# Block 0's constants made by GpSimd, one bias loaded later, and a new order for the prologue's last 382 steps

## The chip, the cores and the metric

The kernel runs on one core of one Trainium2 chip. The metric is the device time of one execution in microseconds (us); the median of three runs stands for it. One execution was also recorded by the hardware profiler, and all rows below come from that one.

## The reference

Two stages follow each other. The first is attention with 4 batches, 8 heads, 768 positions and a head size of 64. A query sees the keys less than 16 positions away, and 24 pooled keys (the maximum over each block of 32 keys, with log 32 added to the score). The pooled values are the means of the same blocks. The second is a gated MLP on the 3072 tokens.

```python
scores_l = scale * q @ k.T            # only |i-j| < 16 is kept
scores_s = scale * q @ k_sum.T + log(32)
a = softmax(concat(scores_l, scores_s))
x = a @ concat(v, v_sum)              # 3072 x 512 after joining the heads
g = x @ w_gate                        # 512 x 1536
out = (silu(g) * (x @ w_val)) @ w_out # 1536 x 512
```

The MLP's weights come as 64-bit floats, and the kernel turns them into 32-bit ones on the chip.

## The kernel before, in words

The 3072 tokens are cut into six blocks of 512. A block's attention is done for four pairs of heads, u = 0 to 3, and its MLP in twelve slices, j = 0 to 11, of 128 hidden channels. A matmul of the MLP is made of three in a rounded format: each factor is split into a high part and a rest, and high x rest, rest x high and high x high are added. So `gate(k,j)` and `val(k,j)` (line 654, tiles g and v) are 12 matmuls of 128x512 each, and `down(k,j)` (line 701, tiles acc) is 12 more.

For each pair, attention is a chain over the engines: `scores` (or `sw` and `sp` in block 0) on TensorE, `ttr0` and `ttr1` (L512, bias and maximum) on VectorE, `exp0` and `exp1` on ScalarE, `rcp` and `nrm` (the division by the sum), `tr0` and `tr1` (L570, transposes on TensorE, against an identity), `pt0` and `pt1` (their copies), `out` (L619, tile xo) on TensorE, `split` on ScalarE and `rest` on VectorE, which make the high part xh and the rest xl for the MLP.

Each weight slice passes through eight steps: `w_load` (DMA), `w_abs` (L217, ScalarE), `w_c1`, `w_c2`, `w_s1`, `w_s2` (L222 to L241, VectorE), `w_hi` (a copy, mostly ScalarE) and `w_lo` (L185, VectorE or GpSimd). "gv" is a slice of w_gate and w_val together, 128x1024; "o" is one of w_out, 128x512.

From start to the end of block 0's MLP the order of all this is written out by hand in the text `PROLOGUE`: 457 steps, each run once, in order. Block 0's attention, the conversion of all weights, block 0's MLP and block 1's attention stand in it. What a step issues goes to the end of its engine's queue, and each engine runs its queue strictly in order. A step's suffix says which engine does it (`=a` ScalarE, `=d` VectorE, `=p` GpSimd), or, for TensorE's steps of block 0, which PSUM pool it takes and how many units of filler matmuls on zeros run ahead of it (`zeros`, L747): `tr0(0,1)=y6` takes the pool psy and runs six units of 128 columns.

PSUM has eight banks in three pools: psg and psy with two each, psc with four. All g and v tiles, and the second score tile of each pair, take their banks from psg, so a third one must wait until a reader has freed the first. The reader of a g is `silu` (ScalarE), of a v it is `mul` (L665, VectorE), and of a score tile `ttr`.

After the prologue a loop over the blocks 1 to 5 goes on in the same way, with no filler.

Two constants matter here. The identity for the transposes comes by DMA in the tile `consts` together with the bias of a sequence's last rows (`cst`, L757). The matrix that forms the means of the values (`mean_sb`, L423) comes at the end of the value load `ve` (L780). The other two biases are built by GpSimd at the start (`make_bias`, L764).

Of the kernel before, what the change touches and what calls it, by code (L numbers as in the profile page):

```python
# [115 lines left out]
w_s1(0,v) w_load(2,gv) w_c1(0,o) w_s2(0,v) w_load(3,gv) w_lo(1,gv)=d w_c2(0,o) out(0,1)=y split(0,0)=a rest(0,0)
w_s1(0,o) pt0(0,3)=a pt1(0,3)=a outp(0,1) w_abs(2,gv) split(0,1)=a w_load(1,o) w_hi(0,v)=a out(0,3)=g outp(0,3)
room(0) rest(0,1) gate(0,0,0) split(0,2)=a gate(0,0,1) rest(0,2) gate(0,0,2) split(0,3)=a rest(0,3) w_c1(2,gv)
w_abs(3,gv) gate(0,0,3) gate(0,1) silu(0,0) w_c1(3,gv) w_c2(2,gv) w_s2(0,o) w_lo(0,v)=p w_s1(2,gv) w_c2(3,gv)
w_s2(2,gv) w_abs(1,o) val(0,0,0) val(0,0,1) silu(0,1) w_hi(0,o)=a val(0,0,2) w_s1(3,gv) w_c1(1,o) val(0,0,3)  # L120
load(1,0) val(0,1) w_hi(2,gv)=a w_lo(2,gv)=d w_load(2,o) w_c2(1,o) mul(0,0) ah(0,0)=a keys(1,0) gate(0,2)
w_abs(2,o) mul(0,1) w_lo(0,o)=d w_s1(1,o) al(0,0)=d ah(0,1)=a w_s2(3,gv) w_load(3,o) w_load(4,gv) silu(0,2)
scores(1,0) down(0,0) val(0,2) w_s2(1,o) w_hi(3,gv)=a al(0,1)=d ttr0(1,0) pool_values(1,0) ttr1(1,0)
w_lo(3,gv)=p w_abs(4,gv) w_abs(3,o) w_c1(4,gv) w_c1(2,o) w_c2(4,gv) gate(0,3) mul(0,2) val(0,3) w_load(5,gv)
w_s1(4,gv) w_c1(3,o) w_s2(4,gv) exp1(1,0) w_hi(1,o)=a w_c2(3,o) w_lo(1,o)=d exp0(1,0) w_hi(4,gv)=a w_s1(3,o)
w_c2(2,o) w_s2(3,o) w_s1(2,o) w_load(7,gv) w_load(6,gv) rcp(1,0) down(0,1) w_lo(4,gv)=d load(1,1) silu(0,3)
w_abs(5,gv) w_hi(3,o)=a w_c1(5,gv) mul(0,3) gate(0,4) val(0,4) ah(0,2)=a w_abs(7,gv) w_c2(5,gv) w_lo(3,o)=d
w_s1(5,gv) w_s2(2,o) nrm(1,0)=a w_hi(2,o)=a w_s2(5,gv) al(0,2)=d w_hi(5,gv)=a tr0(1,0) silu(0,4) w_abs(6,gv)
w_load(4,o) tr1(1,0) pt0(1,0)=a w_abs(4,o) w_lo(2,o)=d pt1(1,0)=a down(0,2) keys(1,1) mul(0,4) w_c1(6,gv)
w_lo(5,gv)=d w_c1(4,o) scores(1,1) ah(0,4)=a w_c2(6,gv) ah(0,3)=a ttr0(1,1) exp0(1,1) ttr1(1,1) al(0,4)=d  # L130
w_load(5,o) load_values(1,0) w_load(7,o) w_load(6,o) w_c1(7,gv) w_s1(6,gv) values(1,0)=a w_load(9,gv) gate(0,5)
al(0,3)=p w_abs(5,o) w_c2(4,o) w_s2(6,gv) w_load(8,gv) w_s1(4,o) val(0,5) w_c2(7,gv) w_hi(6,gv)=a down(0,3)
out(1,0) silu(0,5) w_lo(6,gv)=d w_s2(4,o) w_c1(5,o) w_s1(7,gv) gate(0,6) w_abs(6,o) mul(0,5) w_hi(4,o)=a
w_lo(4,o)=p down(0,4) pool_values(1,1) w_s2(7,gv) w_c2(5,o) load_values(1,1) exp1(1,1) w_c1(6,o) w_s1(5,o)
w_abs(7,o) w_abs(9,gv) w_c1(9,gv) w_c1(7,o) val(0,6) w_hi(7,gv)=a w_lo(7,gv)=d w_c2(9,gv) split(1,0)=a w_s2(5,o)
rcp(1,1) silu(0,6) w_abs(8,gv) w_c2(6,o) w_s1(9,gv) load(1,2) mul(0,6) rest(1,0) w_hi(5,o)=a w_c2(7,o) ah(0,5)=a
values(1,1)=a al(0,5)=p w_load(8,o) w_load(10,gv) w_s1(6,o) gate(0,7) silu(0,7) nrm(1,1)=a w_load(9,o) val(0,7)
w_c1(8,gv) w_lo(5,o)=d w_s2(9,gv) w_hi(9,gv)=a tr0(1,1) down(0,5) mul(0,7) ah(0,7)=a pt0(1,1)=a keys(1,2)
scores(1,2) pool_values(1,2) tr1(1,1) w_lo(9,gv)=d w_s2(6,o) w_abs(8,o) w_s1(7,o) gate(0,9) ttr0(1,2) ttr1(1,2)
pt1(1,1)=a w_c2(8,gv) out(1,1) ah(0,6)=a load(1,3) w_hi(6,o)=a w_lo(6,o)=d exp0(1,2) al(0,6)=p w_s2(7,o)  # L140
w_c1(8,o) exp1(1,2) w_hi(7,o)=a w_s1(8,gv) al(0,7)=d w_s2(8,gv) w_c2(8,o) val(0,9) down(0,6) w_lo(7,o)=d
w_abs(10,gv) w_abs(9,o) w_c1(9,o) w_hi(8,gv)=a w_c1(10,gv) w_lo(8,gv)=d down(0,7) silu(0,9) rcp(1,2) w_c2(10,gv)
w_s1(10,gv) mul(0,9) split(1,1)=a w_s2(10,gv) w_c2(9,o) nrm(1,2)=a gate(0,8) tr0(1,2) w_hi(10,gv)=a keys(1,3)
w_lo(10,gv)=d w_s1(8,o) val(0,8) ah(0,9)=a rest(1,1) room(1) w_load(11,v) w_load(11,g) silu(0,8) mul(0,8)
load_values(1,2) w_load(10,o) w_load(11,o) w_s2(8,o) pt0(1,2)=a al(0,9)=p w_abs(11,v) ah(0,8)=a w_hi(8,o)=a
w_s1(9,o) al(0,8)=d w_lo(8,o)=d gate(0,10) w_c1(11,v) tr1(1,2) pt1(1,2)=a w_c2(11,v) w_s2(9,o) w_s1(11,v)
w_s2(11,v) scores(1,3) ttr0(1,3) values(1,2)=a w_hi(9,o)=a silu(0,10) down(0,8) ttr1(1,3) val(0,10) w_abs(11,g)
w_c1(11,g) w_c2(11,g) w_lo(9,o)=p out(1,2) w_s1(11,g) w_s2(11,g) w_abs(10,o) exp1(1,3) w_hi(11,g)=d w_c1(10,o)
w_hi(11,v)=a down(0,9) w_lo(11,g)=p exp0(1,3) split(1,2)=d mul(0,10) w_lo(11,v)=d w_c2(10,o) rcp(1,3) ah(0,10)=a
rest(1,2) gate(0,11) w_abs(11,o) w_c1(11,o) w_c2(11,o) load_values(1,3) nrm(1,3)=a w_s1(10,o) tr0(1,3)  # L150
# [787 lines left out]
```

## Time and profile before

| | |
|---|---|
| median of 3 runs | 675.41 us (674.69 to 675.70) |
| the profiled execution's own time | 675.49 us |
| its span in the trace | 673.7 us |
| TensorE busy | 667.8 us, 99% |
| VectorE / ScalarE / GpSimd busy | 340.1 / 297.4 / 138.4 us |

The span leaves out 1.8 us of the execution's time. Busy time is a sum over one engine; a busy TensorE may still be one that runs shorter than its best, since the ends of its pipelined matmuls are modelled. In a timeline, start and duration are in us, `x` counts merged instructions, and the bracket is the idle time just before, with what ended it. An fp32 matmul is recorded as two.

### The profile page before, as it was taken

How to read it: one execution, taken by the hardware profiler on the slowest of the kernel's cores; microseconds unless marked ns; L12 is line 12 of the kernel's file. 1: busy time of each engine (PE TensorE's matmuls, PEld its weight loads, DVE VectorE, ACT ScalarE, POOL GpSimd, SP SyncE). 2: the span in 40 equal slices, each digit the busy share in tenths (PEclk: the TensorE clock that was granted, in tenths of full speed). 3: DMA queues.
4: the chain of work that ended last, by engine and by line, in shares of the span. 5: the costliest groups of instructions: out<-in, count | busy, mean ns of one | idle time of the engine just before them, and what ended most of it. 6: DMA issues, size and time to landing. Idle time of an engine off the chain costs nothing.

```text
span 673.7 us, 12397 instructions
## 1 busy us (share of the span) xinstructions
PE 667.8 (99%) x4938; PEld 543.6 (81%) x4938; DVE 340.1 (50%) x952; ACT 297.4 (44%) x729; POOL 138.4 (21%) x131
## 2 busy tenths in 40 slices
...
GB/s 333 332 371 359 41 242 172 51 109 145 56 58 0 56 41 126 84 20 80 103 2 167 52 53 82 12 45 61 59 57 58 0 25 0 63 1 0 1 0 64
DMA packets 72059, 60.37 MB, mean 90 GB/s; under 512 B 42144, under 2 KB 60064, under 8 KB 70464
## 3 DMA queue, kind: packets, MB, share of 16 engines
...
q8 instruction: 39, 0.64, 0.4%
...
## 4 chain that ended last, share of the span: by engine, by line
PE 97%; DVE 2%; DMA 1%; SPq 0%; issue 0%
PE g L654 30%; PE v L654 29%; PE acc L701 29%; PE xo L619 4%; PE sc L454 2%; DMA kq<-in_kF 1%; PE pp L570 1%; DVE p L512 1%; PE sc L465 1%; PE xo L627 1%; DVE ks L343 0%; PE pv L422 0%; PE end L701 0%; PE pp L747 0%; DVE m_g L226 0%
## 5 line engine op out<-in xcount | busy, mean ns | idle before, releaser
L701 PE MATMUL acc<-w_o,ah 128*128 128x512 f32 x572 | 176.2, 389 | 0.0
L654 PE MATMUL g<-xh,w_gv 128*128 128x512 f32 x480 | 159.7, 394 | 0.0
L654 PE MATMUL v<-xh,w_gv 128*128 128x512 f32 x480 | 157.9, 390 | 0.0
L665 DVE TENSOR_TENSOR a<-v,a 128x512 f32<-128x512 f32 x72 | 49.6, 689 | 199.8 <-PE v L654 198.1
L185 POOL TENSOR_TENSOR al<-a,ah 128x512 fp32r<-128x512 f32 x63 | 81.8, 1299 | 328.0 <-ACT ah L189 328.0
L701 PEld LDWEIGHTS acc<-w_o,ah 128*128 128x128 f32 x572 | 107.4, 188 | 22.2
L189 ACT CAST ah<-a 128x512 fp32r<-128x512 f32 x71 | 44.0, 621 | 168.5 <-DVE a L665 168.5
L701 PE MATMUL acc<-w_o,al 128*128 128x512 f32 x286 | 112.0, 392 | 0.0
L654 PEld LDWEIGHTS g<-xh,w_gv 128*128 128x128 f32 x480 | 90.1, 188 | 20.8 <-ACT w_o L189 0.2
L654 PEld LDWEIGHTS v<-xh,w_gv 128*128 128x128 f32 x480 | 90.1, 188 | 18.9
L660 ACT ACTIVATE a<-g 128x512 f32<-128x512 f32 x72 | 43.1, 599 | 134.7 <-PE g L654 131.7
L654 PE MATMUL g<-xl,w_gv 128*128 128x512 f32 x240 | 93.8, 391 | 0.0
L600 DVE STREAM_TRANSPOSE pt_short<-p_short 32x256 f32<-32x256 f32 x192 | 83.8, 436 | 19.8 <-POOL p_short L555 16.9
L654 PE MATMUL v<-xl,w_gv 128*128 128x512 f32 x240 | 93.4, 389 | 0.0
L701 PEld LDWEIGHTS acc<-w_o,al 128*128 128x128 f32 x286 | 53.7, 188 | 11.4 <-DVE al L185 0.2
L654 PEld LDWEIGHTS v<-xl,w_gv 128*128 128x128 f32 x240 | 45.1, 188 | 9.3
L654 PEld LDWEIGHTS g<-xl,w_gv 128*128 128x128 f32 x240 | 45.1, 188 | 8.8
L528 ACT ACTIVATE p_short<-p_short,nm 128x88 f32<-128x88 f32 x128 | 45.3, 356 | 0.2
L185 DVE TENSOR_TENSOR xl<-xo,xh 128x512 fp32r<-128x512 f32 x24 | 16.4, 686 | 57.0 <-ACT xh L189 56.9
L555 POOL TENSOR_TENSOR p_short<-p_short,ri 128x704 f32<-128x704 f32 x16 | 26.0, 1623 | 53.5 <-DVE ri L546 49.6
L654 PE MATMUL g<-xh,w_g 128*128 128x512 f32 x96 | 32.2, 396 | 0.0
L654 PE MATMUL v<-xh,w_v 128*128 128x512 f32 x96 | 31.6, 390 | 0.0
...
## 6 DMA issues: line engine op xcount, KB each, us to landing
raw_gv<-in_wgv SPq DMA_DIRECT2D x10, 1024.0 KB, 11.9
...
```

The costliest lines, as they stand in the source:

```text
L185: (nc.vector if e == "d" else nc.gpsimd).tensor_tensor(out=out, in0=a, in1=b.bitcast(F32), op=ALU.subtract)
L189: nc.scalar.copy(out, in_)
L454: nc.tensor.matmul(sc[h][s * SQ : (s + 1) * SQ, c * SC : (c + 1) * SC], t["q"][hs, i * SQ : (i + 1) * SQ], keys[hs], start=True, stop=True,)
L465: nc.tensor.matmul(sc[h][s * QT : (s + 1) * QT, c * KC : (c + 1) * KC], t["q"][hs, qs], t["kw"][hs, i, :], start=True, stop=True,)
L528: nc.scalar.activation(out=t["p"][:, i, :kc], in_=t["p"][:, i, :kc], func=AF.Exp, scale=-1.0, bias=t["nm"][:, i : i + 1], accum_out=t["sm" ...
L555: (nc.vector if on == "d" else nc.gpsimd).tensor_tensor(out=p, in0=p, in1=ri.rearrange("p (n o) -> p n o", o=1).broadcast_to([P, 2 * NTP, ...
L600: nc.vector.transpose(out=to[r * SQ : (r + 1) * SQ, :, s * SQ : (s + 1) * SQ], in_=t["p"][s * SQ : (s + 1) * SQ, :, at : at + SQ],)
L619: nc.tensor.matmul(ps[hs, qs], vw, t["pt"][:n, h, qs], start=k not in OWN or i == 0, stop=k not in OWN)
L654: nc.tensor.matmul(ps, w[:, cs], x, start=u == 0 and n == 0, stop=u == NP - 1 and n == 2)
L660: nc.scalar.activation(out=a, in_=A.pop(("g", k, j)), func=AF.Silu)
L665: nc.vector.tensor_tensor(out=a, in0=ps, in1=a, op=ALU.mult)
L701: nc.tensor.matmul(out, a[:, ts], w[:, cs], start=begin and n == 0, stop=end and n == 2)
```

## The change

- The identity and the matrix of means are built by GpSimd at the start (`make_consts`: two fills and four selects). `consts` then holds only the last bias by DMA (60 KB in place of 124 KB), and its load is issued far later, behind the loads of slices 1 to 3 of w_out. `ve` loses 112 KB.
- The filler of block 0 goes from 2, 6, 9, 4, 3, 6 units (ahead of `sw(0,0)`, `sw(0,1)`, `tr0(0,2)`, `sw(0,3)`, `tr0(0,0)`, `tr0(0,1)`) to 7, 5, 8, 3, 2, 3.
- From the turns of pair 3 on (`tr1(0,3)`), the 382 steps to the end of the prologue stand in another order, and some change their engine. The steps are the same 457.
- `a_far` can take filler too and `a_max` allocates at whichever half comes first; the lead of a weight tile moves from "v" to "g" of slice 11. Two of the table's rows with filler, before and after, stand at the end of the diff.

```diff
 def w_lead(j, nm):
-    return LEAD if (nm, j) == ("v", NJ - 1) else 0
+    return LEAD if (nm, j) == ("g", NJ - 1) else 0
...
-            t = pro.tile([P, (EVEN + NV - 1) * DM + NV * QC], F32, name="vrows")
+            t = pro.tile([P, (EVEN + NV - 1) * DM], F32, name="vrows")
...
-                    ps[u * QC : (u + 1) * QC, :P], mean_sb[:n, i, :], v_rows()[:n, v_even(i), u * P : (u + 1) * P],
+                    ps[u * QC : (u + 1) * QC, :P], mean_sb[:n, MEAN - i * NS :][:, :QC], v_rows()[:n, v_even(i), u * P : (u + 1) * P],
...
     def load_consts():
-        nonlocal id_sb
-        c = cst.tile([P, KC + P], F32, name="consts")
-        nc.sync.dma_start(c, cst_in)
-        bias_sb[2] = c[:, :KC]
-        id_sb = c[:, KC:]
+        nc.sync.dma_start(bias_sb[2], cst_in)
+
+    def make_pattern(out, value, sign, width):
+        nc.gpsimd.memset(out, value)
+        for x in (-1, 1):
+            nc.gpsimd.affine_select(
+                out=out, in_=out, pattern=[[-x * sign, out.shape[1]]], base=x * width[0] + (x < 0) * (width[1] - 1),
+                channel_multiplier=x, compare_op=ALU.is_ge, fill=0.0,
+            )
+
+    def make_consts():
+        nonlocal id_sb, mean_sb
+        c = cst.tile([P, KC + P], F32, name="consts")
+        bias_sb[2] = c[:, :KC]
+        id_sb = c[:, KC:]
+        make_pattern(id_sb, 1.0, 1, (0, 1))
+        mean_sb = pro.tile([P, MEAN + QC], F32, name="mean")
+        make_pattern(mean_sb, 1.0 / BLK, BLK, (BLK * MEAN - WIN, BLK))
...
     make_bias()
+    make_consts()
...
-rcp(0,3) tr1(0,0)=y nrm(0,1)=p tr0(0,1)=y6 w_s1(1,gv) tr1(0,1)=c nrm(0,3)=d w_s2(1,gv) fv()=g pt1(0,2)=a
+nrm(0,1)=p tr0(0,1)=y3 w_s1(1,gv) tr1(0,1)=c nrm(0,3)=d w_s2(1,gv) fv()=g pt1(0,2)=a w_load(0,v) out(0,2)=c
```

**TensorE, the first MLP blocks and block 1's first scores.** Before, four gate and value blocks and a fifth, g_2, stood ahead of the scores `sc_1_0` (sc0 and sc1 alternate; the second row is sc1, which takes its bank from psg). The bracket names the engines that the instruction waits for.

```order
L654 MATMUL g_0_596<-xh_0_550,w_g_509 128x512 [waits DVE_49,PE_49]
...
L654 MATMUL g_1_620<-xh_0_550,w_gv_522 128x512 [waits PE_49]
...
L654 MATMUL v_0_644<-xh_0_550,w_v_567 128x512 [waits Activation_49,Pool_49]
...
L654 MATMUL v_1_673<-xh_0_550,w_gv_522 128x512 [waits Activation_49]
...
L654 MATMUL g_2_699<-xh_0_550,w_gv_686 128x512 [waits DVE_49]
...
L465 MATMUL sc_1_0_728<-kw_0_668,q_0_665 64x120 [waits DMAHW4_49,DMAHW2_49,Pool_49]
L465 MATMUL sc_1_0_729<-kw_0_668,q_0_665 64x120 [waits DVE_49]
```

Now:

```order
L650 MATMUL v_0_612<-xh_0_548,w_v_578 128x512 [waits DVE_49,PE_49]
...
L650 MATMUL g_0_622<-xh_0_548,w_g_580 128x512 [waits DVE_49,Pool_49]
...
L650 MATMUL g_1_666<-xh_0_548,w_gv_512 128x512 [waits Activation_49]
...
L458 MATMUL sc_1_0_679<-kw_0_607,q_0_604 64x120 [waits DMAHW3_49,DMAHW1_49,Pool_49]
L458 MATMUL sc_1_0_680<-kw_0_607,q_0_604 64x120 [waits DVE_49]
...
L650 MATMUL v_1_712<-xh_0_548,w_gv_512 128x512 [waits Activation_49]
...
L650 MATMUL v_3_733<-xh_0_548,w_gv_710 128x512 [waits DVE_49,PE_49]
```

The scores have moved up from the sixth place to the fourth, directly behind v_0, g_0 and g_1; sc1 now takes the bank of v_0, and v_3 the bank of sc1.

**VectorE, from the last `rest` of block 0 to the first `mul`.** Before:

```order
L185 TENSOR_TENSOR xl_3_611<-xo_3_569,xh_3_610 128x512
L222 TENSOR_SCALAR m_gv_560<-m_gv_560 128x1024
L222 TENSOR_SCALAR m_gv_615<-m_gv_615 128x1024
L226 TENSOR_SCALAR m_gv_560<-m_gv_560 128x1024
L241 SCALAR_TENSOR_TENSOR m_o_512<-raw_o_503,m_o_512 128x512
L234 SCALAR_TENSOR_TENSOR m_gv_560<-raw_gv_525,m_gv_560 128x1024
...
L185 TENSOR_TENSOR w_gv_686<-m_gv_560,w_gv_686 128x1024
L226 TENSOR_SCALAR m_o_642<-m_o_642 128x512
L665 TENSOR_TENSOR a_0_633<-v_0_644,a_0_633 128x512
```

Now, from the cast of w_v's slice 0 (the three `rest` left out, of xl_0, xl_2 and xl_1, are like the one shown):

```order
L184 CAST w_v_578<-m_v_510 128x512
L178 TENSOR_TENSOR w_v_578<-m_v_510,w_v_578 128x512
...
L178 TENSOR_TENSOR xl_3_617<-xo_3_561,xh_3_616 128x512
L215 TENSOR_SCALAR m_gv_589<-m_gv_589 128x1024
L219 TENSOR_SCALAR m_gv_589<-m_gv_589 128x1024
L227 SCALAR_TENSOR_TENSOR m_gv_589<-raw_gv_539,m_gv_589 128x1024
L234 SCALAR_TENSOR_TENSOR m_gv_589<-raw_gv_539,m_gv_589 128x1024
L215 TENSOR_SCALAR m_o_642<-m_o_642 128x512
L219 TENSOR_SCALAR m_o_642<-m_o_642 128x512
L336 TENSOR_REDUCE ks_663<-kt_0_602 128x24
L227 SCALAR_TENSOR_TENSOR m_gv_583<-raw_gv_515,m_gv_583 128x1024
L661 TENSOR_TENSOR a_0_698<-v_0_612,a_0_698 128x512
```

The cast and the rest of w_v's slice 0 have come to VectorE, block 1's key reduction (ks) stands ahead of the first `mul` (the last row), and slice 3 of "gv" (m_gv_589) runs ahead of slice 2 (m_gv_583).

## Rows read from the trace of the kernel before

**Rows 1.** The page's first part: busy time, share of the span, instructions.

```profile
PE 667.8 (99%) x4938; PEld 543.6 (81%) x4938; DVE 340.1 (50%) x952; ACT 297.4 (44%) x729; POOL 138.4 (21%) x131
```

**Rows 2.** Busy time by stretch: PE, PEld, DVE, ACT, POOL, PEclk, DMA share, GB/s.

```profile
40.00:50.00 10.00, 10.00 (x72) 8.00 (x71) 10.00 (x22) 5.59 (x8) 1.45 (x2) 1.00 1.01 422
```

**Rows 3.** Timeline of TensorE up to the first gate block: start, us.

```profile
6.44 0.70 PE L747 MATMUL sc<-warm 128*128 128x256 f32 x2
8.07 0.89 PE L479 MATMUL sc<-kq 64*64 64x96 f32 x32 [0.93 <-DMA kq<-in_kF]
...
14.34 1.04 PE L570 MATMUL pp<-consts,p 128*120 128x128 f32 x8
...
19.55 1.53 PE L747 MATMUL pp<-warm 128*128 128x512 f32 x4 [0.34 <-DVE nm L512]
20.91 1.04 PE L570 MATMUL pp<-consts,p 128*120 128x128 f32 x8
...
23.68 1.15 PE L619 MATMUL xo<-pt,vrows 96*64 96x64 f32 x32
...
32.53 0.50 PE L654 MATMUL g<-xh,w_g 128*128 128x512 f32 x1
```

**Rows 4.** Timeline of ScalarE behind the value means.

```profile
23.81 1.07 ACT L189 COPY vs<-pv 24x128 f32<-24x128 f32 x4 [0.93 <-PE pv L422]
```

**Rows 5.** DMA issues: KB each, us from issue to landing; and one issue's start.

```profile
vrows<-in_vO SPq DMA_DIRECT2D x1, 1024.0 KB, 15.3
...
7.95 0.33 SPq L791 DMA_DIRECT2D vrows<-in_vO  x1
```

**Rows 6.** Timeline of GpSimd: the biases at the start, and a later division.

```profile
1.57 1.60 POOL L773 TENSOR_SCALAR_AFFINE_SELECT bias<-bias 64x192 f32<-64x192 f32 x4
...
17.97 1.79 POOL L555 TENSOR_TENSOR p<-p,ri 128x960 f32<-128x960 f32 x1 [1.50 <-DVE ri L546]
```

**Rows 7.** Timeline of VectorE between 19 and 50 us.

```profile
19.32 0.99 DVE L241 SCALAR_TENSOR_TENSOR m_g<-raw_g,m_g 128x512 int32<-128x512 int32 x1
...
26.60 0.43 DVE L222 TENSOR_SCALAR m_v<-m_v 128x512 f32<-128x512 f32 x1 [1.35 <-ACT m_v L217]
27.06 0.43 DVE L226 TENSOR_SCALAR m_v<-m_v 128x512 int32<-128x512 int32 x1
...
36.76 1.22 DVE L234 SCALAR_TENSOR_TENSOR m_gv<-raw_gv,m_gv 128x1024 int32<-128x1024 int32 x1
37.90 0.68 DVE L226 TENSOR_SCALAR m_gv<-m_gv 128x1024 int32<-128x1024 int32 x1
...
42.57 0.68 DVE L665 TENSOR_TENSOR a<-v,a 128x512 f32<-128x512 f32 x1
43.17 0.94 DVE L343 TENSOR_REDUCE ks<-kt 128x24 f32<-128x768 f32 x1
44.03 0.68 DVE L665 TENSOR_TENSOR a<-v,a 128x512 f32<-128x512 f32 x1
...
48.77 0.28 DVE L512 CUSTOM_DVE_ANT_0 p<-sc,bias 128x120 f32<-128x120 f32 x1
...
49.58 0.95 DVE L363 TENSOR_REDUCE vr<-vt 128x24 f32<-128x768 f32 x1
```

**Rows 8.** Timeline of TensorE from the fourth block on; last, a piece of the chain.

```profile
40.84 0.39 PE L654 MATMUL v<-xh,w_gv 128*128 128x512 f32 x1
...
46.05 0.39 PE L654 MATMUL g<-xh,w_gv 128*128 128x512 f32 x1
46.37 1.05 PE L465 MATMUL sc<-kw,q 64*64 64x120 f32 x32
47.35 0.50 PE L701 MATMUL acc<-w_o,al 128*128 128x512 f32 x1
47.70 0.64 PE L701 MATMUL acc<-w_o,ah 128*128 128x512 f32 x2
...
156.85 2.72 PE acc L701 x12
```

More of the change, by code (lines that the diff above doesn't have):

```diff
@@ L116 @@
[L116 to L150, printed above, removed]
@@ new lines @@
+cst() val(0,0,2) w_abs(4,gv) w_s2(3,gv) w_c1(0,o) val(0,0,3) w_c2(0,o) keys(1,0) gate(0,1) scores(1,0)
+w_s1(2,gv) silu(0,0) mul(0,0) w_load(6,gv) silu(0,1) w_s1(0,o) load_values(1,0) w_s2(0,o) w_hi(3,gv)=a val(0,1)
+w_abs(1,o) ah(0,0)=a w_s2(2,gv) w_hi(0,o)=a w_lo(3,gv)=d val(0,3) ttr1(1,0) w_load(8,gv) al(0,0)=d
+pool_values(1,0) w_abs(2,o) w_hi(2,gv)=a mul(0,1) w_lo(0,o)=p ttr0(1,0) exp1(1,0) w_c1(4,gv) exp0(1,0)
+w_c2(4,gv) w_c1(1,o) gate(0,3) w_abs(3,o) w_c2(1,o) down(0,0) w_c1(3,o) w_s1(1,o) w_s2(1,o) w_load(7,gv)
@@ new lines @@
+load(1,1) w_c1(2,o) w_c2(2,o) w_s1(4,gv) w_load(5,gv) ah(0,1)=a silu(0,3) rcp(1,0) w_abs(7,gv) w_s2(4,gv)
+w_lo(2,gv)=p w_hi(1,o)=a mul(0,3) nrm(1,0)=a w_s1(2,o) gate(0,2) al(0,1)=d w_hi(4,gv)=a w_lo(1,o)=d w_lo(4,gv)=d
+silu(0,2) val(0,2) w_s2(2,o) keys(1,1) w_load(6,o) tr0(1,0) w_load(9,gv) mul(0,2) ah(0,3)=a w_abs(5,gv)
+w_abs(6,gv) values(1,0)=a w_c1(5,gv) w_c2(3,o) w_c2(5,gv) w_s1(3,o) down(0,1) w_s1(5,gv) ah(0,2)=a gate(0,4)
+w_load(10,gv) silu(0,4) val(0,4) tr1(1,0) w_hi(2,o)=a w_c1(6,gv) al(0,2)=d w_load(4,o) scores(1,1) w_c2(6,gv)
@@ new lines @@
+w_s1(4,o) rcp(1,1) w_c1(9,gv) w_s2(4,o) val(0,6) w_abs(5,o) w_lo(7,gv)=d ah(0,5)=a silu(0,6) w_load(10,o)
+w_c1(6,o) al(0,5)=d w_hi(4,o)=a nrm(1,1)=a w_c2(9,gv) val(0,7) w_c1(5,o) tr1(1,1) keys(1,2) w_c1(8,gv)
+pt1(1,1)=a values(1,1)=a mul(0,6) w_c2(5,o) w_s1(5,o) w_lo(4,o)=d gate(0,7) w_abs(10,gv) w_s2(5,o) w_s1(9,gv)
+w_c2(6,o) silu(0,7) w_s2(9,gv) w_s1(6,o) w_abs(8,o) w_hi(9,gv)=a w_hi(5,o)=a w_s2(6,o) down(0,4) tr0(1,1)
+scores(1,2) w_lo(9,gv)=d pt0(1,1)=a mul(0,7) w_load(7,o) ah(0,6)=a ttr0(1,2) out(1,1) w_abs(7,o) w_c1(10,gv)
@@ new lines @@
+w_lo(10,gv)=p w_c2(10,o) rest(1,1) mul(0,9) pool_values(1,2) room(1) scores(1,3) mul(0,8) w_lo(8,o)=d w_c1(9,o)
+tr1(1,2) ttr0(1,3) ah(0,9)=a ttr1(1,3) w_c2(9,o) ah(0,8)=a gate(0,10) w_load(11,g) w_s1(9,o) w_s2(9,o)
+w_s1(10,o) w_abs(11,g) w_c1(11,g) pt1(1,2)=a w_load(11,o) exp0(1,3) w_c2(11,g) w_s1(11,g) w_s2(11,g) al(0,8)=p
+exp1(1,3) w_hi(9,o)=a val(0,10) w_load(11,v) rcp(1,3) silu(0,10) nrm(1,3)=d w_lo(9,o)=d down(0,8) w_abs(11,v)
+tr1(1,3) al(0,9)=d w_hi(11,g)=a w_c1(11,v) values(1,2)=a out(1,2) w_c2(11,v) down(0,9) tr0(1,3) mul(0,10)
```

58 lines of the change are left out of this document (35 added, 23 removed).

## The prediction

> **What bounds the kernel now.** I began with the page's busy times: TensorE 667.8 us of a span of 673.7 us [rows 1]. No other engine is above half, so time can be won only where TensorE waits, or works on something that nobody needs, and lost only where a new wait appears. The stretches tell where one may appear: from 40 to 50 us VectorE is busy for all of the ten microseconds, too [rows 2]. There the MLP blocks of TensorE and the weight conversion of VectorE run side by side, and the reader should see that TensorE has company at the limit. Behind the prologue the order is the same in both kernels, so only the first 145 us or so can differ.
>
> The timeline of TensorE then shows what the start waits for. The scores of pair 0 wait for keys by DMA until 8.07 us, after 0.93 us of idleness; the filler of pair 1's turns starts at 19.55 us, after 0.34 us in which it waits for VectorE's maxima (the last reader of its bank); from there to the first gate block, at 32.53 us, no wait is shown [rows 3]. All sums below are against the profiled execution, 675.49 us, which is 0.08 us above the median of the three runs, 675.41.
>
> **The constants by GpSimd.** Four selects of 64x192 take 1.60 us in all, 0.40 each [rows 6]. Four more with at most 128 elements a partition cost 1.6 us at most, so GpSimd ends its constants before 6 us. The first transposes that read the identity run at 14.34 us, and the means of the values, four matmuls behind the last transposes at 20.91 us, end in time for ScalarE's copy at 23.81 us [rows 3, 4]; so eight microseconds of other work hide the constants: cost nothing. Without that cover every transpose of block 0 would be late. What they save lies in the DMA queue: the 124 KB of `cst` leave its front (60 of them come again far behind), and `ve` loses 112 KB. The odd values stand behind both issues, so 124 + 112 = 236 KB less stand in front of them. At the 422 GB/s of a full stretch [rows 2] that is 0.6 us. The odd values landed at 7.95 + 15.3 = 23.25 us [rows 5], and the first `out` started at 23.68 us [rows 3]: a slack of 0.43 us, so that without this part nothing behind could come more than 0.43 us earlier.
>
> **The filler.** Six units took from 19.55 to 20.91 us, 0.227 us each [rows 3]. The five units added ahead of `sw(0,0)` fit: 6.44 + 7 x 0.227 = 8.03 us, before the keys at 8.07 us. The four units dropped between there and 19.55 us win nothing, since the wait for VectorE ends when it did: VectorE's order up to there is the same, and the idleness in front of it grows from 0.34 us to about a microsecond. The three units dropped behind 19.55 us do count: 3 x 0.227 = 0.68 us. ScalarE takes this up, as it waited 0.93 us for the means [rows 4]; so does the first `out`, at 23.00 us, behind values at 22.65 us. **Term: -0.68 us**, and the first MLP block starts at 31.85 us in place of 32.53.
>
> **The new order: a wait at the first scores.** The first score matmul into psg now stands behind three blocks of 12, and takes the bank of v_0, so it waits for `mul(0,0)` on VectorE. I add up VectorE's queue from `w_c1(0,v)`, which waited for ScalarE at 26.60 us [rows 7] and so comes at 25.92 us. There are 22 instructions to the end of that `mul`. An instruction whose successor reads its result costs its duration and 0.03 us (0.43 to 0.46, from 26.60 to 27.06); one that is followed by independent work costs less: 0.60 us for 128x512 with two operands (42.57 to 43.17), 1.14 us for 128x1024 (36.76 to 37.90), 0.86 us for the keys' maxima (43.17 to 44.03) [rows 7].
>
> - four of 128x512 with one operand, each with a dependent successor (two w_c1, a w_c2, the cast): 4 x 0.46 = 1.84, and one without: 0.34;
> - seven at 0.60 (w_s1 and w_lo of v's slice 0, four `rest`, w_c2 of slice 2): 4.20;
> - four of about 0.69 with a dependent successor: 4 x 0.72 = 2.88;
> - three at 1.14 = 3.42, and w_s1 of slice 3 with its dependent successor, 1.25;
> - the keys' maxima 0.86, the `mul` itself 0.68.
>
> That is 15.47 us, to 41.39 us. One thing more: `w_lo(0,g)` goes to GpSimd and runs beside `w_lo(0,v)` on VectorE. A 128x512 instruction with two operands took 0.99 us at 19.32 us, while GpSimd's division ran from 17.97 to 19.76 us, against 0.68 elsewhere [rows 6, 7]. I take these 0.31 us: 41.70 us. The Trainium skill says why, in its GPSIMD Engine Reference (Specifications): GpSimd shares its SBUF interfaces with VectorE, and they contend when VectorE runs a two-port mode or reads two SBUF inputs. By that rule every VectorE instruction with two inputs beside a division of GpSimd is slowed, and the row with 0.99 agrees.
>
> TensorE reaches the scores at 31.85 + (40.84 - 32.53) + 0.09 = 40.25 us [rows 3, 8]. **Term: +1.4 us.** Bounds: if every successor overlaps fully (nine dependent ones by 0.1 each), VectorE is 0.9 us faster, and without the contention's 0.3 that leaves +0.2; if the cast and one more neighbour are slowed like the 0.99 row, 2 x 0.31 = 0.6 more: +2.0. I stay near the middle because the rows of dependent pairs speak against the low end.
>
> **A second wait, at v_3.** The scores take 0.98 us (46.37 to 47.35), `v_1` behind them 2.84 us with the entry of 0.12: TensorE is at v_3 at 45.5 us [rows 8]. Its bank is that of the scores, read by four `ttr`. From the start of `mul`, at 41.0 us, VectorE has 0.60, 0.72, 0.60, 1.14 and 1.14 us (the `mul`, w_s1 and w_s2 of w_out, w_s2 of slice 2, w_lo of slice 3), then four at 0.20 (48.77 to 49.58) and the last reading: 46.1 us [rows 7]. **Term: +0.6 us**, between 0 and 1.
>
> **Fewer changes between kinds of matmul.** Each group of attention's small matmuls between MLP blocks costs at its edges: 46.05 + 0.227 to 46.37 is 0.09 us, and 47.35 to 47.70 is 0.12 us more than a matmul's 0.227 (2.72 us for twelve), 0.21 us in all [rows 8]. Before, block 1's attention stands in 14 such groups, now in 10: four edges fewer, at most 0.84 us. Not every edge costs as much; I take 0.15 each. **Term: -0.6 us**, between -0.84 and 0.
>
> **The rest of the prologue.** Behind 46 us the table moves 7.0 us of work to VectorE and 6.1 us from it (rests, casts, one division and one copy, by the prices above). The needs behind are blocks that TensorE reaches 0.1 to 1 us after VectorE's own sum, so I take nothing; without that cover it is 0.9 us, the net. The loads of slice 4 of "gv" now run ahead of slice 0 of w_out and of block 1's keys; nothing needs those keys before the scores at 40 us, so I count this at nothing and keep its opposite as a rival.
>
> The sum: -0.68 + 1.4 + 0.6 - 0.6 = +0.7 us, so **676.2 us**. About 0.2% (1.35 us) is what a measurement of this kernel can tell from no change.
>
> **Rivals.**
>
> 1. The waits hardly come, since VectorE reaches `mul(0,0)` by 40.5 us. Then the gain stays: -0.68 - 0.84 + 0.2 = -1.3 us, 674.2 us. For it: no place in the trace before shows VectorE making TensorE wait behind 20 us. Against: this order asks for the first `mul` 2 us earlier and puts the keys' maxima in front of it.
> 2. VectorE becomes the bound for the whole prologue: lateness at 46 us is not caught up, since the queue stays full [rows 2], and the 0.9 us that it gains on balance shows up as waits before w_lo of slices 8 and 11. With half of the larger contention that is +0.7 + 0.9 + 0.3 = +1.9 us, 677.4 us, slower. It decides from 0.65 us of further waits on.
> 3. The weights and keys, in their new order of loading, land after 41 us, and the scores wait for DMA: a microsecond more, 677.2 us. Against: before, the scores at 46.37 us waited for nothing by DMA [rows 8], and 236 KB less stand in the queue.
> 4. The change doesn't do what it says (the constants are late, or VectorE's early chain is not what ends the wait at 19.55 us): then the first term is zero or positive, and the result near 677 us.
>
> **How the numbers follow.** My forecast has 0.53, the rivals 0.22, 0.18, 0.04 and 0.03. Faster by over 0.2% needs nearly all of rival 1, or more saved at edges than I count: 0.18. Slower takes rivals 2 to 4 and the upper part of my own case: 0.27. Within 0.2%: 0.55. The range goes from rival 1 to just above rival 2: 674.2 to 677.6 us.
>
> **What would show it.** In the profile after: pair 1's turns at about 20.2 us and the first v matmul at about 31.9 us (first term); the scores of block 1 stretched, with an idle time of about a microsecond ended by VectorE's `mul`, near 41.7 us; v_3 starting near 46.1 us on VectorE's `ttr`; no idle time of TensorE above 0.3 us behind it; v_11 ending near 138 us. No wait at 41 us would make the forecast wrong on the fast side, waits at g_8 or g_11 on the slow side.

## The result and the profile after

The changed kernel takes 679.84 us (median of 4 runs, 679.68 to 683.39) against 675.5 us for the kernel before. The quotient of the medians is 1.0064; the ratio over all runs, the long one among them, is 1.0073, with an interval of 1.0059 to 1.0087. The forecast was 676.2 us with a range up to 677.6; the kernel is slower by 4.3 us in the medians, and the loss is larger than any case of the prediction allowed. The profiled execution took 679.89 us, with a span of 678.2 us. The one run of 683.39 us had a mean granted clock of 0.996 where the others had 1.0; the experiments come back to that.

The first part of the profile's page and one stretch of the windows view, which answer to [rows 1, 2] (busy time of TensorE, its weight loads, VectorE, ScalarE and GpSimd; then the granted clock, DMA share and GB/s):

```profile
PE 668.3 (99%) x4936; PEld 544.2 (80%) x4936; DVE 341.3 (50%) x954; ACT 291.1 (43%) x718; POOL 142.8 (21%) x137
```

```profile
40.00:50.00 10.00, 9.50 (x69) 7.33 (x68) 9.97 (x27) 7.95 (x19) 5.86 (x4) 1.00 1.04 351
```

TensorE's busy time has hardly grown (667.8 to 668.3), so most of the time went into waits. In the stretch from 40 to 50 us VectorE is as full as before, and GpSimd has 5.86 us of work there where it had 1.45. The list of TensorE's waits names the rest (engine, line, what it waited for; us in total, times, longest):

```profile
PE xo L615 <- ACT vs L395: 1.9, 1, 1.9
PE warm L743 <- DVE warm L819: 1.5, 1, 1.5
PE pp L743 <- DVE nm L508: 1.1, 1, 1.1
PE g L650 <- DVE xl L178: 1.0, 1, 1.0
PE v L650 <- DVE nm L508: 0.5, 1, 0.5
```

The wait at `warm` was there before, and the one at `pp` (1.1 us in place of 0.3) stands where filler was dropped. Three are new, 1.9, 1.0 and 0.5 us. (`nm` is the reading of VectorE's maxima, `vs` the pooled values.) Their places in TensorE's timeline, with what answers to [rows 3, 8] around them:

```profile
4.82 1.56 PE L472 MATMUL sc<-kq 64*64 64x96 f32 x32
...
7.09 1.77 PE L743 MATMUL sc<-warm 128*128 128x512 f32 x4
8.79 0.89 PE L472 MATMUL sc<-kq 64*64 64x96 f32 x32
...
19.94 0.88 PE L743 MATMUL pp<-warm 128*128 128x384 f32 x2 [1.11 <-DVE nm L508]
...
23.43 1.15 PE L615 MATMUL xo<-pt,vrows 96*64 96x64 f32 x32
...
32.27 0.50 PE L650 MATMUL v<-xh,w_v 128*128 128x512 f32 x1
...
34.24 0.47 PE L650 MATMUL g<-xh,w_g 128*128 128x512 f32 x1 [1.01 <-DVE xl L178]
...
41.60 0.39 PE L650 MATMUL g<-xh,w_gv 128*128 128x512 f32 x1
41.91 1.11 PE L458 MATMUL sc<-kw,q 64*64 64x120 f32 x32
...
46.48 0.47 PE L650 MATMUL v<-xh,w_gv 128*128 128x512 f32 x1 [0.50 <-DVE nm L508]
...
129.35 0.27 PE L394 MATMUL pv<-consts,vr 128*24 128x128 f32 x1
131.54 1.33 PE L615 MATMUL xo<-pt,vw 120*64 120x64 f32 x32 [1.92 <-ACT vs L395]
...
148.47 0.39 PE L650 MATMUL g<-xh,w_g 128*128 128x512 f32 x1
...
674.12 0.27 PE L697 MATMUL end<-w_o,al 128*128 128x192 f32 x1
```

Of the kernel before, the rows that answer to the first and to the last two of these:

```profile
4.81 1.27 PE L479 MATMUL sc<-kq 64*64 64x96 f32 x32
...
144.68 0.39 PE L654 MATMUL g<-xh,w_g 128*128 128x512 f32 x1
...
670.29 0.27 PE L701 MATMUL end<-w_o,al 128*128 128x192 f32 x1
```

And VectorE, which answers to [rows 7], on the way to the first `mul` (L661) and to the maxima (L508):

```profile
33.41 1.28 DVE L178 TENSOR_TENSOR xl<-xo,xh 128x512 fp32r<-128x512 f32 x2
...
41.25 0.68 DVE L661 TENSOR_TENSOR a<-v,a 128x512 f32<-128x512 f32 x1
...
44.31 1.22 DVE L178 TENSOR_TENSOR w_gv<-m_gv,w_gv 128x1024 fp32r<-128x1024 f32 x1
45.44 0.28 DVE L508 CUSTOM_DVE_ANT_0 p<-sc,bias 128x120 f32<-128x120 f32 x1
```

**Where the 4.4 us of the span are** (678.15 us, before 673.71). The first MLP block starts at 32.27 us, 0.26 earlier [rows 3]. Block 1's first gate block starts at 148.47 in place of 144.68 us, and from there to TensorE's last matmul both kernels take the same (525.65 us, before 525.61). Between the two lies the stretch that the new order fills, 116.20 us against 112.15: 1.01 + 0.50 + 1.92 = 3.43 us of waits, and 0.62 us by which the same matmuls took longer. Another 0.61 us come behind TensorE: from the start of its last matmul (674.12, before 670.29) to the end of the span it is 4.03 us, before 3.42. The last two stores take longer (DMA issues: KB, us to landing):

```profile
out<-o_end SPq DMA_DIRECT2D x1, 160.0 KB, 2.6
...
out<-o_end SPq DMA_DIRECT2D x1, 96.0 KB, 2.3
```

Before, the same two took 1.8 and 1.7 us. So -0.26 + 3.43 + 0.62 + 0.61 = 4.40 us, and 0.04 in the loop.

### The profile page after: what moved, and what is told of

The parts are those of the page before. It is cut to its first block, busy times and chain, and to the rows that moved or that the text cites. A ratio compares the mean times of both kernels' runs of the same rounds, so it can differ in the third digit from the quotient of the medians.

```text
span 678.2 us, 12397 instructions
## 1 busy us (share of the span) xinstructions
PE 668.3 (99%) x4936; PEld 544.2 (80%) x4936; DVE 341.3 (50%) x954; ACT 291.1 (43%) x718; POOL 142.8 (21%) x137
## 3 DMA queue, kind: packets, MB, share of 16 engines
HBM read 53.08 MB, written 6.29 MB: 88 GB/s over the span
## 4 chain that ended last, share of the span: by engine, by line
PE 94%; DVE 4%; ACT 1%; issue 0%; DVEq 0%; ACTq 0%
PE acc L697 29%; PE g L650 29%; PE v L650 28%; PE xo L615 3%; PE sc L447 2%; DVE p L508 1%; PE pp L566 1%; PE warm L743 0%; PE sc L458 0%; DVE m_gv L227 0%; DVE xl L178 0%; DVE m_gv L234 0%; PE sc L472 0%; DVE w_gv L178 0%; PE pv L415 0%
## 5 line engine op out<-in xcount | busy, mean ns | idle before, releaser
L661 DVE TENSOR_TENSOR a<-v,a 128x512 f32<-128x512 f32 x72 | 49.6, 688 | 199.8 <-PE v L650 197.3
L178 POOL TENSOR_TENSOR al<-a,ah 128x512 fp32r<-128x512 f32 x62 | 80.1, 1292 | 323.2 <-ACT ah L182 323.2
```

The costliest lines, as they stand in the source:

```text
L178: (nc.vector if e == "d" else nc.gpsimd).tensor_tensor(out=out, in0=a, in1=b.bitcast(F32), op=ALU.subtract)
L661: nc.vector.tensor_tensor(out=a, in0=ps, in1=a, op=ALU.mult)
```

## The experiments

Each ratio is against runs of the kernel before on the same chip, whose medians were between 674.93 and 675.52 us; the rows of one chip compare best with each other (chip 13: busy, rest1_first, relief2; chip 1: old_fill_early, rest1_hi, relief3; the other eight ran on chip 3).

| kernel | us | ratio | interval |
|---|---|---|---|
| constants alone (const_only) | 675.58 | 1.0003 | 0.9994 to 1.0012 |
| constants and filler (const_fill) | 675.16 | 0.9994 | 0.9985 to 1.0003 |
| three units less (fill3) | 674.89 | 0.9990 | 0.9981 to 0.9998 |
| six units less (fill0) | 674.74 | 0.9989 | 0.9980 to 0.9998 |
| the change, early values (values_early) | 678.15 | 1.0040 | 1.0027 to 1.0052 |
| the change, old filler (old_fill) | 681.42 | 1.0087 | 1.0073 to 1.0101 |
| old filler and early values (old_fill_early) | 678.07 | 1.0052 | 1.0035 to 1.0069 |
| old filler, matmuls in the wait (busy) | 683.39 | 1.0122 | 1.0107 to 1.0137 |
| four rests first (rests_first) | 681.17 | 1.0086 | 1.0072 to 1.0099 |
| one rest first (rest1_first) | 679.96 | 1.0068 | 1.0053 to 1.0083 |
| one rest first, GpSimd later (rest1_hi) | 677.18 | 1.0033 | 1.0021 to 1.0045 |
| non-urgent steps later (relief) | 682.31 | 1.0101 | 1.0088 to 1.0115 |
| the same without GpSimd (relief2) | 680.51 | 1.0078 | 1.0061 to 1.0095 |
| and the second `mul` earlier (relief3) | 682.2 | 1.0109 | 1.0094 to 1.0124 |

### The change in parts

The order of before, with GpSimd's constants; `cst()` stands behind `w_load(2,o)`:

```diff
-sw(0,0)=yg2 sp(0,0) kq(1) cst() kq(3)
+sw(0,0)=yg2 sp(0,0) kq(1) kq(3)
...
+w_load(2,o) cst()
```

> Order and filler of before; only the constants come from GpSimd and the last bias is loaded later. Theory A (the constants are hidden, as the prediction had it): 675.5 us, within 0.4. Rival B (the changed start is itself dear: in the changed kernel the first score matmuls took 1.56 and 1.01 us where they took 1.27 and 0.62 before, so TensorE came to its full rate later): up to 0.7 us more, 676.2, and the first scores show the longer durations here too.

675.58 us, no difference: the constants are hidden, as the prediction had it. The score matmuls of the start did take 1.56 and 0.83 us, but the keys by DMA come at 8.07 us all the same, and a wait of 0.46 us in front of them takes it up. Then the filler of the change as well:

> The same, with the filler counts of the change as well; only the order from pair 3's turns on is that of before. Theory A: the first term of the prediction alone, -0.68 us, 674.8 us. Rival B (seven units ahead of the first scores of pair 0 make VectorE 0.4 us later, as in the profile after): -0.26 us, 675.2 us. Either way the new order would hold 4.6 to 5.0 us of loss.

```diff
-sw(0,0)=yg2
-sw(0,1)=yg6
+sw(0,0)=yg7
+sw(0,1)=yg5
...
-tr0(0,1)=y6
+tr0(0,1)=y3
```

675.16 us. The interval holds theory A and rival B (674.8 and 675.2 us), so the run doesn't decide between them. Either way what is left of the change, the order from pair 3's turns on, holds the whole loss. To see the filler term without the seven units ahead of pair 0's scores, only the six units behind the wait at 19.55 us were cut:

```diff
-tr0(0,1)=y6
+tr0(0,1)=y3
```

> Order of before with GpSimd's constants, and of the filler only the six units behind the wait at 19.55 us cut to three; all the others as before, so that TensorE still meets the keys at 8.07 us. Theory A (the prediction's first term, clean of the seven units ahead of pair 0's scores): -0.68 us against the 675.58 of the constants alone, 674.9 us, first gate block at 31.85 us. Rival B (ScalarE's copies or the odd values hold the first out): 675.4 us, with a wait at out.

674.89 us, against 675.58 for the constants alone, as theory A had it. The trace agrees: from pair 0's scores (8.43 us) to the first gate block (32.22) it takes 23.79 us, and before 24.46 (8.07 to 32.53), which is 0.67 less. So the term has its size when the filler ahead of pair 0 stays as it was. With `tr0(0,1)=y`:

> The same with none of the six units. Theory A: the next limit is ScalarE's copy of the means and the odd values (22.7 us by the queue's 422 GB/s), which leaves 0.2 to 0.4 us more than with three units, 674.5 to 674.7 us, with a wait at out. Rival B (every unit cut is won): 1.36 us, 674.2 us.

674.74 us. TensorE's timeline there shows the next limit, and it is GpSimd's division of pair 1, not the odd values that I had expected:

```profile
20.13 1.09 PE L566 MATMUL pp<-consts,p 128*120 128x128 f32 x8 [0.60 <-POOL p L551]
```

These two are the versions that beat the kernel before, by 0.6 to 0.8 us; the intervals leave out 1 only just. The stretch from the first MLP block to block 1's first gate block takes 112.12 to 112.16 us in these four kernels, as before (112.15): the changed kernel's 116.20 come from the order, with the lead of the weight tile that belongs to it.

### The wait near 130 us

ScalarE's timeline of the changed kernel shows what stood ahead of the pooled values (`vs`) that TensorE waited for:

```profile
128.26 0.60 ACT L656 ACTIVATE a<-g 128x512 f32<-128x512 f32 x1
129.38 0.67 ACT L210 ACTIVATE m_v<-raw_v 128x512 f32<-128x512 f32 x1 [0.52 <-DVE w_o L178]
129.96 0.60 ACT L182 CAST w_g<-m_g 128x512 fp32r<-128x512 f32 x1
130.58 0.61 ACT L182 COPY vw<-vs 24x512 f32<-24x512 f32 x1
131.23 0.27 ACT L395 ACTIVATE vs<-pv 24x128 f32<-24x128 f32 x1
```

`w_abs(11,v)` (L210) waited 0.52 us for VectorE's rest of slice 9 of w_out, which the change had taken from GpSimd, and the values stood behind it and two more steps. One step moved:

```diff
-exp1(1,3) w_hi(9,o)=a val(0,10) w_load(11,v) rcp(1,3) silu(0,10) nrm(1,3)=d
+exp1(1,3) w_hi(9,o)=a val(0,10) w_load(11,v) rcp(1,3) silu(0,10) values(1,2)=a nrm(1,3)=d
...
-tr1(1,3) al(0,9)=d w_hi(11,g)=a w_c1(11,v) values(1,2)=a out(1,2)
+tr1(1,3) al(0,9)=d w_hi(11,g)=a w_c1(11,v) out(1,2)
```

> The changed kernel with one step moved: the pooled values of pair 2 of block 1 now stand on ScalarE directly behind silu of slice 10, ahead of the absolute value of slice 11's v and the high part of its g, and on TensorE ahead of down of slice 8. Theory A (the 1.92 us wait at 129.6 us is made by ScalarE's order alone): the wait goes with its restart costs, -1.9 to -2.3 us, 677.5 to 677.9 us. Rival B (VectorE is the bound of the stretch, and the lateness only shows there): the wait turns up again at g or v of slice 11, and the gain is under 0.8 us, 679.0 us or more.

678.15 us, 1.69 less, between theory A and rival B. The waits that are left there:

```profile
PE v L650 <- DVE w_v L178: 0.3, 1, 0.3
PE xo L615 <- ACT vs L395: 0.2, 1, 0.2
```

So ScalarE's order made the wait: 0.23 us of it is left, and 0.29 us came up at v of slice 11. The two profiled executions (679.89 and 677.56 us) differ by more than the step is worth. In the stretch from the first MLP block to block 1's first gate block the trace has 1.08 us less (115.12 in place of 116.20). Ahead of it, where the two programs are the same, this execution was 0.65 us earlier:

```profile
5.08 0.95 PE L472 MATMUL sc<-kq 64*64 64x96 f32 x32 [0.20 <-DMA kq<-in_qF]
...
31.62 0.50 PE L650 MATMUL v<-xh,w_v 128*128 128x512 f32 x1
```

Behind TensorE's last matmul, where they are the same too, it was 0.70 us shorter (3.33 in place of 4.03), and that stays unexplained. The step itself brought about 1.1 us.

### The filler, and the clock behind a wait

The changed kernel with the filler counts of before:

```diff
-sw(0,0)=yg7
-sw(0,1)=yg5
+sw(0,0)=yg2
+sw(0,1)=yg6
...
-tr0(0,1)=y3
+tr0(0,1)=y6
```

> The changed kernel with the filler counts of before (2, 6, 9, 4, 3, 6 units). Theory A (the lower filler brought 0.26 us at the first MLP block, and what follows waits for VectorE anyway): between 679.8 and 680.1 us, first v block at 32.5 us. Rival B (seven units ahead of the first scores make VectorE's whole queue 0.4 us later, and that lateness is carried to the waits at g_0 and v_3): 679.4 us, and the wait at g_0 shrinks.

681.42 us, above what theory A and rival B gave. The waits are those of the changed kernel, but the windows view (stretch, its length, TensorE's busy time and instructions, granted clock, DMA share, GB/s) shows a lower clock behind the wait of 1.92 us:

```profile
128.00:130.00 2.00, 1.95 (x12) 1.00 0.00 0
130.00:132.00 2.00, 0.13 (x4) 1.00 0.03 8
132.00:134.00 2.00, 2.00 (x33) 0.62 0.00 0
134.00:136.00 2.00, 2.00 (x6) 0.53 0.55 161
136.00:138.00 2.00, 2.00 (x13) 1.00 0.14 35
```

TensorE was idle for nearly the whole stretch from 130 to 132 us, and in the next four the granted clock is near half of full speed, the lower of its two levels, 1.2 GHz. In the changed kernel the same wait of 1.92 us left the clock at 1.00. The Trainium skill says in TensorE: Matmul & The Clock Gate (What's actually happening) that a gate sets the clock by how busy the engine has been recently; the rows above agree, and that it can go either way after one and the same wait is what these two kernels show. The stretch from the first MLP block to block 1's first gate block takes 117.73 us here, 1.53 more than in the changed kernel. The four executions point the same way: three with a mean granted clock of 0.997 took 681.34 to 682.23 us, and one with 0.999 took 680.07, where theory A had put it. The changed kernel's run of 683.39 us, with 0.996, may be of this kind; it left no trace. To tell the clock from the filler itself, the early values were put into this kernel:

> The kernel with the early values (678.15 us) with the filler counts of before. Theory A (old_fill's 1.3 us above its expected 680.1 were the clock's fall behind the wait near 130 us): without the wait no fall, 678.3 to 678.8 us. Rival B (the larger filler itself makes the kernel dearer): 679.5 us or more.

678.07 us, a ratio of 1.0052: the fall of the clock is gone with the wait, and the larger filler costs nothing that these intervals show against 1.0040. The stretch takes 115.10 us, with the change's filler 115.12. An earlier attempt had put nine matmuls on the identity in front of `out(1,2)`, to keep TensorE busy through the wait:

```diff
-out(1,2)
+out(1,2)=y9
...
+            for _ in range(int(on[1:] or 0)):
+                nc.tensor.matmul(ps[:, :P], id_sb, id_sb, start=True, stop=True)
```

> The kernel with the change's order and the filler counts of before (681.42 us), and nine 128-column matmuls on the identity ahead of out of pair 2 of block 1, in TensorE's wait of 1.92 us near 130 us; they are overwritten. Theory A (its 1.3 us over the expected 680.1 come from the granted clock, 0.62 and 0.53 in the 4 us behind the wait): no drop of the clock, 680.0 to 680.3 us. Rival B (the 1.3 us have another cause): 681.3 us or more.

683.39 us. It tells nothing of the question: the nine took the same bank as `out`, waited for the same ScalarE instruction, and ran behind the wait instead of in it.

### The waits at g_0 and v_3

g_0's first matmul reads only pair 0's tiles, which were ready. What it waited for, at 34.24 us, is its bank: `out(0,1)` has gone from psy to psg, its last reader is `rest(0,1)` on VectorE, and this stands behind two steps of slice 2 of "gv". First both late rests were moved ahead of these:

```diff
-val(0,0,0) split(0,3)=a w_c1(2,gv) w_load(1,o) gate(0,0,0) w_load(3,o) w_c2(2,gv) rest(0,1) gate(0,0,1) gate(0,0,2) rest(0,3)
+val(0,0,0) split(0,3)=a w_load(1,o) gate(0,0,0) w_load(3,o) rest(0,1) gate(0,0,1) gate(0,0,2) rest(0,3) w_c1(2,gv) w_c2(2,gv)
```

> The kernel with the early values (678.15 us), and on VectorE the first two steps of slice 2 of gv moved behind the last two rests of block 0, for which g_0 waited 1.01 us. Theory A (VectorE's whole queue up to the first mul is late, and g_0 only shows it): the same 1.47 us of VectorE's work still stand ahead of mul(0,0), so the wait of 1.01 us moves to the first scores and the time stays, 677.8 to 678.5 us. Rival B (the rests are simply in the wrong place): the wait goes and does not come back, 677.1 us.

681.17 us, worse than theory A and rival B had it. `rest(0,3)` now waits 0.63 us for ScalarE with VectorE's whole queue behind it; counted from the first MLP block, `mul(0,0)` starts 0.6 us later than in the changed kernel (9.61 against 8.98 us). VectorE's rest of slice 3 of "gv" then takes 2.31 us in place of 1.22, for the reason that the next run shows, and v_3 waits 2.46 us, with the clock at 0.58 behind it. So only `rest(0,1)` was moved:

```diff
-w_c1(2,gv) w_load(1,o) gate(0,0,0) w_load(3,o) w_c2(2,gv) rest(0,1)
+rest(0,1) w_c1(2,gv) w_load(1,o) gate(0,0,0) w_load(3,o) w_c2(2,gv)
```

> The kernel with the early values (678.15 us), and on VectorE only the rest of pair 1 moved ahead of the first two steps of slice 2 of gv; that of pair 3, whose high part ScalarE gives late, stays behind them. Theory A (VectorE's sum up to the first mul bounds the first MLP blocks, and the wait shows at whatever asks first): the 1.0 us at g_0 turns into 1.0 us at the first scores, 677.9 to 678.4 us. Rival B (two separate losses): 677.1 us.

679.96 us. The wait at g_0 is gone. 0.34 us appear at the scores, ended by ScalarE's silu and not by VectorE's `mul`, so the second score tile has another bank there. But v_3 waits 2.12 us. The next two fences are VectorE and GpSimd of this kernel at that place:

```profile
44.10 2.32 DVE L178 TENSOR_TENSOR w_gv<-m_gv,w_gv 128x1024 fp32r<-128x1024 f32 x1
```

```profile
43.84 1.50 POOL L178 TENSOR_TENSOR w_o<-m_o,w_o 128x512 fp32r<-128x512 f32 x1 [2.59 <-ACT w_o L182]
```

VectorE's instruction takes 2.32 us in place of 1.22. GpSimd's had started 0.26 us earlier and ended at 45.34; 1.24 us in front of that and about 1.1 behind it make the 2.32. To reverse who starts first, one ScalarE step was moved, on which GpSimd's instruction depends:

```diff
-w_hi(0,o)=a w_lo(3,gv)=d val(0,3) ttr1(1,0) w_load(8,gv) al(0,0)=d pool_values(1,0) w_abs(2,o)
+w_lo(3,gv)=d val(0,3) ttr1(1,0) w_load(8,gv) al(0,0)=d pool_values(1,0) w_abs(2,o) w_hi(0,o)=a
```

> rest1_first (679.96 us) with one ScalarE step moved: the high part of slice 0 of w_out behind the absolute value of slice 2 of w_out. In rest1_first GpSimd's rest of slice 0 of w_out started 0.26 us before VectorE's rest of slice 3 of gv, which then took 2.32 us; now GpSimd's comes 0.6 us later. Theory A (whichever of the two starts first shuts the other out): VectorE's instruction takes 1.2 us again, the wait at v_3 falls from 2.1 to about 1.0 us or less, 678.2 to 678.9 us. Rival B (the lateness has another cause): 679.8 us or more.

677.18 us. VectorE starts first, takes its usual time, and now GpSimd's instruction is the longer one (2.00 us in place of 1.50, and of 1.27 in the kernel relief below):

```profile
43.90 1.22 DVE L178 TENSOR_TENSOR w_gv<-m_gv,w_gv 128x1024 fp32r<-128x1024 f32 x1
```

```profile
44.24 2.00 POOL L178 TENSOR_TENSOR w_o<-m_o,w_o 128x512 fp32r<-128x512 f32 x1 [3.19 <-ACT w_o L182]
```

The waits are now 0.34 us at the scores and 0.98 at v_3, 1.32 in sum where the kernel with the early values had 1.51; the ratio of 1.0033 lies within its interval. Without the wait at g_0, v_3 still starts 14.11 us behind the first MLP block, where the changed kernel has 14.21. That fits theory A of the one rest first: VectorE's sum up to 46 us bounds this stretch, and moving one rest moves the wait.

Three attempts to shorten that sum failed. In the first, on top of the four rests, `mul(0,0)` went ahead of `w_s1(2,gv)`, the four steps of slice 0 of w_out behind `ttr1(1,0)`, and GpSimd's rest of slice 2 of gv ahead of that of w_out:

```diff
-w_c1(0,o) val(0,0,3) w_c2(0,o) keys(1,0) gate(0,1) scores(1,0) w_s1(2,gv) silu(0,0) mul(0,0)
+val(0,0,3) keys(1,0) gate(0,1) scores(1,0) silu(0,0) mul(0,0) w_s1(2,gv)
...
+ttr1(1,0) w_c1(0,o) w_c2(0,o) w_s1(0,o) w_s2(0,o)
```

> The same, and further: on VectorE the mul stands ahead of the third step of slice 2, and the four steps of slice 0 of w_out (2.1 us, not needed before down at 52 us) behind the maxima of block 1's pair 0; on GpSimd the rest of slice 2 of gv stands ahead of that of slice 0 of w_out. Theory A (non-urgent work ahead of the urgent on VectorE makes the waits at g_0 and v_3): both go, -1.0 and -0.5 us with their restart costs, 676.4 to 676.8 us. Rival B (VectorE's queue is full to 130 us, so any lateness only moves on): the waits come back at down_0, g_2 or g_4, 677.7 us or more.

682.31 us. The wait at g_0 goes and v_3's falls to 0.39 us, but a VectorE instruction of 0.43 us met GpSimd's rest of slice 2 (44.99 to 47.55 us):

```profile
45.33 2.51 DVE L219 TENSOR_SCALAR m_o<-m_o 128x512 int32<-128x512 int32 x1
```

```profile
44.99 2.56 POOL L178 TENSOR_TENSOR w_gv<-m_gv,w_gv 128x1024 fp32r<-128x1024 f32 x1 [4.64 <-ACT w_gv L182]
```

It ends 0.3 us behind GpSimd's, and TensorE waited 3.30 us at g_3, whose bank `mul(0,1)` frees. The second took over these moves on VectorE, but with one rest first, and put both of GpSimd's instructions on VectorE as well:

```diff
-w_lo(2,gv)=p
-w_lo(0,o)=p
+w_c2(0,o) w_lo(2,gv)=d w_s1(0,o) w_s2(0,o) w_hi(0,o)=a
+w_lo(0,o)=d
```

> The same, with mul(0,0) ahead of the third step of slice 2, the four steps of slice 0 of w_out behind the maxima of block 1's pair 0, and the rests of slice 2 of gv and of slice 0 of w_out on VectorE instead of GpSimd, so that no GpSimd instruction runs beside them. Theory A (work that was not urgent, and GpSimd's instructions that shut VectorE out, made the waits at g_0 and v_3): both go, and the 1.9 us more on VectorE are taken up later, 676.4 to 676.9 us. Rival B (VectorE is full to 130 us): the waits come back by slice 11, 677.7 us or more.

680.51 us: the waits at g_0 and v_3 are gone, and g_3 (the next expectation calls it g_2) waits 2.25 us for `mul(0,1)`. The third moved that `mul` up, and the pooled maxima of the values behind `w_lo(0,o)`:

```diff
-w_c2(0,o) w_lo(2,gv)=d w_s1(0,o)
+w_c2(0,o) w_lo(2,gv)=d mul(0,1) w_s1(0,o)
```

> relief2 (680.51 us) with mul(0,1) moved up directly behind the rest of slice 2 of gv, and the pooled maxima of the values behind the rest of slice 0 of w_out. Theory A (relief2's wait of 2.25 us at g_2 was mul(0,1)'s place): the wait goes, with the clock's fall behind it, and so do those at g_0 and v_3: 676.4 to 677.2 us. Rival B (VectorE is full to 130 us): a wait of 1 us or more comes back elsewhere, 677.7 us or more.

682.2 us. Now the wait is 4.03 us, for ScalarE's silu, which stands behind work that waits for VectorE:

```profile
PE g L650 <- ACT a L656: 4.0, 1, 4.0
```

If VectorE is full to 130 us, the rival theory of all three, these are what one would see; but each of the three orders also has a conflict of its own, and an order without one could still exist. Whether the early loss can be won back without another one stays open. The share of the clock is open there, too: relief2's four executions took 680.38 to 680.64 us, and the one whose mean granted clock was 0.997, the others having 1.0, was the shortest.

## Why the prediction was wrong

- **Constants at nothing:** right. GpSimd's last select ends before 5 us, the kernel with the constants alone takes the same time, and the odd values landed at 6.29 + 16.1 = 22.4 us (22.65 forecast).
- **The filler, -0.68:** -0.26. The step that failed is 6.44 + 7 x 0.227 = 8.03 us. The filler began at 7.09 us and took 0.24 us a unit, so pair 0's scores came at 8.79 us, behind the keys. VectorE's maxima, which follow TensorE's scores, were 0.4 us later by 19.9 us. The 6.44 was the value of one execution. The score matmuls ahead of the filler took 1.27 us there and 1.56 us here, and 0.95 us in the kernel with the early values, the same program up to there: it reached pair 0's scores at 8.10 us and the first MLP block at 31.62, 0.91 us earlier than the kernel before. So how much of this term shows is partly luck. Before, a wait of 0.93 us for the keys took such differences up; the seven units leave no such slack. The three units less behind 19.55 us were worth their price, as the run with three units less showed.
- **The wait at the first scores, +1.4:** 1.01 us, but at g_0, for a bank of whose move from psy to psg I took no account; that left no wait at the scores, which started at 41.91 us, while the first `mul` ended at 41.93 (forecast: 41.70). That VectorE's sum came so near is partly luck. Its queue started at 26.33 us in place of 25.92, its 22 instructions took 15.60 us where 15.47 were priced, and the 0.31 us for GpSimd's company never came on VectorE: `w_lo(0,v)` started first and took its usual time, and GpSimd's `w_lo(0,g)` beside it took 1.76 us, where a rest of this size took 1.31 before.

```profile
26.33 0.43 DVE L215 TENSOR_SCALAR m_v<-m_v 128x512 f32<-128x512 f32 x1 [0.68 <-ACT m_v L210]
...
30.18 0.69 DVE L178 TENSOR_TENSOR w_v<-m_v,w_v 128x512 fp32r<-128x512 f32 x1
```

```profile
30.25 1.76 POOL L178 TENSOR_TENSOR w_g<-m_g,w_g 128x512 fp32r<-128x512 f32 x1 [10.09 <-ACT w_g L182]
```

- **The wait at v_3, +0.6:** 0.50 us.
- **Fewer changes between kinds, -0.6:** the same matmuls took 0.62 us more. The edges that I counted did go: by the starts of the matmuls, going into and out of attention's groups cost 1.73 us before (14 groups) and 1.16 now (10 groups), beyond the 0.23 us of a matmul of the MLP: 0.57 less. Two things were left out. Groups that are joined keep their edges inside: there are nine (1.51 us) where there were five (0.89), beside the one with the wait. For example, four transposes took 0.35 us ahead of an MLP matmul before (94.73 to 95.08) and take 0.53 ahead of scores now (69.10 to 69.63). And the matmuls on both sides of the three new waits take 0.6 us more than the waiting itself: from g_0's predecessor to g_0, for one, it is 1.40 us, of which 1.01 is the wait and a matmul's step 0.23.

```profile
94.73 0.60 PE L570 MATMUL pp<-consts,p 128*120 128x128 f32 x4
95.08 0.47 PE L701 MATMUL acc<-w_o,al 128*128 128x512 f32 x1
```

```profile
69.10 0.60 PE L566 MATMUL pp<-consts,p 128*120 128x128 f32 x4
69.63 1.05 PE L458 MATMUL sc<-kw,q 64*64 64x120 f32 x32
```

- **The rest of the prologue, 0:** 1.92 us of wait. This is the step that cost most: "The needs behind are blocks that TensorE reaches 0.1 to 1 us after VectorE's own sum, so I take nothing". I went along the blocks that read weights and along VectorE alone. The wait arose at attention's values, on ScalarE, behind three steps of which the first waited for a rest that had moved to VectorE. My second rival had the direction (lateness of VectorE that shows late in the prologue) and 0.9 us for it; its sign, a wait for a weight of slice 11, came only to 0.29 us, and only once the values stood earlier.
- **Behind TensorE's last matmul:** 0.61 us that no term names. The program is the same there, and its cause stays open.
- **Rival 3, keys and weights late by DMA:** no wait of TensorE for a DMA shows in the changed kernel.

The sums: forecast -0.68 + 1.4 + 0.6 - 0.6 = +0.7; measured -0.26 + 1.01 + 0.50 + 0.62 + 1.92 + 0.61 = +4.4.
